# Attention output transposed by DMA from SBUF to SBUF, with the k and q loads placed behind it

## The chip, the cores and the metric

One core of a Trainium2 chip. The metric is the device time of one execution in microseconds (us). Engines: PE is TensorE, ACT ScalarE, DVE VectorE, POOL GpSimd, SP SyncE. Inputs and outputs lie in HBM, the tiles in SBUF, and matmuls write into PSUM. Spans are from one profiled execution of each kernel and lie up to 2 us below the device time of the same run. The granted clock is the share of its full clock that PE was given, 1.000 at most. "SPq" is SyncE as it issues DMAs. The chain is the work that ended last, followed back from the last instruction, at each step to what it had waited for.

## The reference, cut to what matters

```python
# 8 batches, 8 heads, 576 positions, head size 64; model 512, hidden 2048
scores = q @ k.T / 8 + bias[head, i - j]            # by distance; one value from |i - j| of about 128 on
attn   = softmax(scores)                            # 576 x 576 per head
x      = (attn @ v) as [batch * position, head * 64]     # 4608 x 512
h      = x @ w_in;  g = h + sin(alpha * h)**2 / alpha    # 4608 x 2048
out    = g @ w_out                                       # 4608 x 512
```

The kernel treats a batch as four pairs of heads, and the MoE part as nine blocks of 512 tokens. Batch t's attention and block t's MoE alternate.

## The kernel before

The first MoE product contracts over the model dimension, so x has to lie transposed, as `xT`, with the model dimension on partitions. The kernel makes it for each pair and each of two windows of positions (384 and 192): normalise on DVE (`xn`), transpose on PE into PSUM (`turn`), copy to `xT` on DVE or ACT (`put`).

```python
    XN = 1536                       # xT is a ring of 1536 token columns
    xT = sgl.tile([128, NP, XN], F16, name="xT")
    ...
        def turn(e):
            tr.v = new_av().bitcast(F16)
            for i, qc in enumerate(QC[w]):
                nc.tensor.transpose(out=tr.v[:, qc - q0 : qc - q0 + 128],
                                    in_=xn.v[:, i], identity=id_sb)
        ...
        def put(e):                 # PSUM -> xT, at (S * t + q0) % XN
            ...
```

k and q of the batches 2 to 7 are first cast by POOL's DMA into HBM ("staging"), then read back transposed by SyncE's DMA, a whole batch ahead of their use. k goes through `kraw` and from there, in four plain copies, to `kz` and `kt`.

```python
    def load_kqT(t):
        nc.sync.dma_start_transpose(out=kraw[:, :, :], in_=staged_k.ap()[t])
        kz = kzs[t % 2]
        nc.sync.dma_start(out=kz[0:64, :, 0:S], in_=kraw[0:64, :, :])
        nc.sync.dma_start(out=kz[64:128, :, S : 2 * S], in_=kraw[64:128, :, :])
        ...                         # two small copies to kts
        nc.sync.dma_start_transpose(out=qTs[t % 2][:, :, :], in_=staged_q.ap()[t])
    ...
        def first(t=t):             # with the first QK matmul of batch t
            if 1 <= t < T - 1:
                load_v16(t + 1)
                load_kqT(t + 1)
```

A scheduler in the program (`Plan`) fixes the order of every engine when the program is built, from its own table of durations. The second MoE product ("mo", 64 matmuls a block) is filler: the scheduler puts it where PE would wait, with a quota inside attention (`QUOTA = 48`, `OFFSET = 8`). On the chip every engine keeps the fixed order: PE's 3379 instructions in the experiments ring and ring_whole below, whose loads differ, come in the same order, one for one.

The softmax here doesn't subtract the row's maximum and nothing guards it: scores larger than these inputs give would overflow.

Of the kernel before, what the change touches and what calls it, by code (L numbers as in the profile page):

```python
# [24 lines left out]
def t_act(n):  # L25
    return n / 1200.0 + 0.052
# [4 lines left out]


D_TBL = 1.285
LAT = {"PE": 0.2, "ACT": 0.18, "DVE": 0.18, "POOL": 0.2, "DMA": 0.0}
NBUF = {"sc": 4, "av": 2, "mo": 2, "u": 2, "g": 2, "s16": 3, "sq": 3, "outs": 5, "xn": 3}


class Task:
    def __init__(self, engs, emit, deps, pri, nb=0.0):
        self.engs, self.emit, self.deps, self.pri, self.nb = engs, emit, list(deps), pri, nb  # L40
        self.allocs = []
        self.s_only = self.fill = False
        self.end = self.eng = None


class Buf:
# [8 lines left out]
class Plan:  # L55
# [18 lines left out]
    def ready(self, t):  # L74
        r = t.nb
        for d in t.after:
            if d.end is None:
                return None
        for d in t.deps:
            if d.end is None:  # L80
                return None
            r = max(r, d.end - (LAT["PE"] if d.eng == "PE" and "PE" in t.engs else 0.0))
        taken = {}
        for b in t.allocs:
            ring, n = self.rings[b.tag], NBUF[b.tag]
            k = taken[b.tag] = taken.get(b.tag, -1) + 1
            if len(ring) + k >= n:
                for x in ring[k - n].users:
                    if x.end is None:
                        return None  # L90
                    r = max(r, x.end)
        return r

    def run(self, t0):
        free = {e: t0 for e in ("PE", "ACT", "DVE", "POOL")}
        todo = list(self.tasks)
        while todo:
            best = None
            cands = {e: [] for e in free}
            look = 0  # L100
            for t in todo:
                look += 1
                if look > WINDOW:
                    break
                r = self.ready(t)
                if r is None:
                    continue
                for e in t.engs:
                    if e == "ACT" and t.s_only and not self.sin:
                        continue  # L110
                    st = max(free[e], r)
                    if t.fill:
                        if self.in_qk and self.used >= OFFSET + QUOTA * self.share:
                            continue
                        cands[e].append((st + FILL_GAP, t))
                    else:
                        cands[e].append((st, t))
            for e, c in cands.items():
                if not c:
                    continue  # L120
                s0 = min(x[0] for x in c)
                st, t = min(((x[0], x[1]) for x in c if x[0] <= s0 + SLACK[e]),
                            key=lambda x: (x[1].pri, x[0]))
                fin = st + t.engs[e]
                if best is None or (st, fin) < best[:2]:
                    best = (st, fin, e, t)
            st, fin, e, t = best
            if e == "PE" and self.warm is not None and free[e] < WARM_END:
                ring = self.rings["mo"][-2:]
                b = Buf("mo")  # L130
                x = Task({}, None, [], 0)
                b.users.append(x)
                if st > free[e] + 0.5 and len(ring) == 2 and all(
                    y.end is not None and y.end <= free[e] for y in ring[0].users
                ):
                    self.warm()
                    free[e] += 0.43
                    x.end, x.eng = free[e], e
                    self.rings["mo"].append(b)
                    continue  # L140
            if t.fill:
                self.used += 1
                st -= FILL_GAP
                fin -= FILL_GAP
            for b in t.allocs:
                self.rings[b.tag].append(b)
            t.emit(e)
            t.end, t.eng = fin + LAT[e], e
            free[e] = fin
            todo.remove(t)  # L150
        self.made = max(free.values())
# [12 lines left out]
T_TR1 = (38.5, 38.5)  # L164
T_W = 30.0
T_WO = 54.0
WARM0 = 6
WARM1 = 1
AV_PRI = 250
NORM_PRI = -300  # L170
CP_PRI = -1
SIN_SET = "trig_and_small"
SLACK = {"PE": 0.02, "ACT": 0.02, "DVE": 0.02, "POOL": 0.02}



# [11 lines left out]
def kernel(  # L188
# [11 lines left out]
    nc = tc.nc  # L200
    T, H, S, D = q.shape
# [11 lines left out]
    XN = 1536  # L213
# [8 lines left out]
    staged_k = nc.dram_tensor("staged_k", [T, S, H * D], F16, kind="Internal")  # L222
    staged_q = nc.dram_tensor("staged_q", [T, S, H * D], F16, kind="Internal")
# [112 lines left out]
                in_=src[t].rearrange("h s d -> s h d"),  # L336
            )

    def load_kqT(t):
        nc.sync.dma_start_transpose(out=kraw[:, :, :], in_=staged_k.ap()[t])  # L340
        kz = kzs[t % 2]
        nc.sync.dma_start(out=kz[0:64, :, 0:S], in_=kraw[0:64, :, :])
        nc.sync.dma_start(out=kz[64:128, :, S : 2 * S], in_=kraw[64:128, :, :])
        for z in range(2):
            r = slice(64 * z, 64 * z + 64)
            nc.sync.dma_start(out=kts[t % 2][r, :, r], in_=kraw[r, :, 512:S])
        nc.sync.dma_start_transpose(out=qTs[t % 2][:, :, :], in_=staged_q.ap()[t])

    def load_v16(t):
        vp = v[t].rearrange("h s d -> s h d")  # L350
# [76 lines left out]
    def load_mhr(eng):  # L427
# [12 lines left out]
        out=tabL,  # L440
# [107 lines left out]
    def plan_alpha():  # L548
# [13 lines left out]
        m = plan.add({"PE": 0.1}, mm, [], 5000, nb=20.0, new=[b])  # L562
        return plan.add({"DVE": 0.4}, cp, [m], 5000, use=[b])

    def plan_pair(t, p, kqt, tails, first, gate, ub):

        u = Cell()
# [3 lines left out]
        for i, (kind, c) in enumerate(units):  # L571
# [39 lines left out]
                         after=head, new=b + ([ub] if i == 0 else []))  # L611
            head = head or [m]
            x = plan.add({"ACT": t_act(n)}, ex, [m] + gate, base + 20, use=b + [ub])
            if kind == 1:

                def bh(e):
                    io = u.v[:, 8, 384:576]
                    nc.vector.tensor_tensor(out=io, in0=io, in1=mh[:, p, 0:192], op=ALU.mult)

                done[(0, 4)] = x  # L620
                done[(1, 4)] = plan.add({"DVE": 0.19}, bh, [x], base + 10,
                                         nb=0.0 if t else T_MH[p > 0], use=[ub])
                continue
# [22 lines left out]
    def plan_av(t, p, w, u, ub, done):  # L646
# [35 lines left out]

        x = plan.add({"DVE": 0.4 + n / 960.0}, norm, prev, base + NORM_PRI, new=[xb], use=[ab])

        def turn(e):
            tr.v = new_av().bitcast(F16)
            for i, qc in enumerate(QC[w]):
                nc.tensor.transpose(  # L688
                    out=tr.v[:, qc - q0 : qc - q0 + 128], in_=xn.v[:, i], identity=id_sb
                )  # L690
# [1 line left out]
        x = plan.add({"PE": 0.06 * nq}, turn, [x], base + NORM_PRI, new=[tb], use=[xb])  # L692

        def put(e):
            x0 = (S * t + q0) % XN
            for a, m in ((0, min(n, XN - x0)), (min(n, XN - x0), n)):
                if a < m:
                    copy_on(e, xT[:, p, (x0 + a) % XN : (x0 + a) % XN + m - a], tr.v[:, a:m])
# [97 lines left out]
    for t in range(T):  # L796
        PB = 1000000 * t

        def first(t=t):
            if 1 <= t < T - 1:  # L800
                load_v16(t + 1)
                load_kqT(t + 1)
            if t + 2 < T:
                stage_kq(t + 2)

        if t > 0:
            gate = [plan.add({"ACT": D_TBL}, lambda e: set_table(EXP_SET), sins, PB)]
        exps = []
        for p in range(NP):
            ub = Buf("u")  # L810
            if t == 0 and p + 1 < NP:
                for kq in range(2):
                    tr[(0, p + 1, kq)] = plan_tr(0, p + 1, kq, 100 * (16 * p + 8), T_PAIR[p][kq])
            kqt = tr[(t, p, 0)][0] + tr[(t, p, 1)][0] if t < 2 else []
            tails = tr[(t, p, 0)][1] if t < 2 else []
            u, done = plan_pair(t, p, kqt + pe_gate, tails, first, gate, ub)
            exps.extend(x for x in plan.tasks[-40:] if x.engs.keys() == {"ACT"})
            for w in range(2):
                xdone.setdefault((t, w), []).extend(plan_av(t, p, w, u, ub, done))
        if t == 0:  # L820
            for p in range(NP):
                for kq in range(2):
                    tr[(1, p, kq)] = plan_tr(1, p, kq, 20000 + 10 * p, T_TR1[kq])
        tbl = [plan.add({"ACT": D_TBL}, lambda e: set_table(SIN_SET), exps, PB)]
        sins = []
        for b in [t] if t < T - 1 else [t, t + 1]:
            m, s_ = plan_moe_in(b, tbl)
            sins += s_
        pe_gate = [m]
        for b in [t] if t < T - 1 else [t, t + 1]:  # L830
            for a in range(4):
                plan_mo(b, a)
# [33 lines left out]
```

## Time and profile before

| | before |
|---|---|
| device time, median of 2 | 416.26 us (414.1 to 418.43) |
| profiled span (of a further run, 412.09 us) | 410.3 us |
| PE, ACT, DVE busy | 96%, 82%, 71% |
| period of a batch (first MoE matmul to first MoE matmul, mean over batches 2 to 7) | 43.8 us |
| mean granted PE clock | 1.000 |

### The profile page before, as it was taken

The numbers are of one execution on the slowest core, as the hardware profiler recorded it, in microseconds if no ns is written. First come the engines' busy times: TensorE is split into PE (matmuls) and PEld (weight loads), VectorE is DVE, ScalarE is ACT, GpSimd is POOL, SyncE is SP. The second block draws the span as 40 slices with busy tenths as digits, with TensorE's granted clock in tenths as the row PEclk, the third lists the DMA queues.
The fourth block names the chain that finished last, engine by engine and source line by source line (L and its number), as shares of the span: only waits on it lengthen the run. The fifth ranks groups of instructions, "written<-read, shape, count | busy, mean of one in ns | idle before, by whom it ended". The sixth has DMA issues, their size and how long they took to land.

```text
span 410.3 us, 8747 instructions
## 1 busy us (share of the span) xinstructions
PE 395.4 (96%) x3519; PEld 227.5 (55%) x3519; DVE 289.7 (71%) x683; ACT 337.3 (82%) x502; POOL 85.6 (21%) x98
## 2 busy tenths in 40 slices
PE   4897999999999999999999999999999999999996
PEld 1474446754576447744665467645764477444442
DVE  5895996749666976688576956696768766799200
ACT  2877988879988998889888998799979988899311
POOL 7863952044000900071004400120000000000000
PEclk9999999999999999999999999999999999999999
DMA  9899999949900995099906990293000000000111
GB/s 170 189 206 219 205 162 158 216 89 164 185 28 29 155 182 94 27 135 165 131 28 104 161 142 27 69 169 79 27 28 27 26 27 27 28 1 0 53 77 77
DMA packets 135145, 41.90 MB, mean 102 GB/s; under 512 B 121209, under 2 KB 129489, under 8 KB 135105
## 3 DMA queue, kind: packets, MB, share of 16 engines
q0 software_dynamic: 89872, 19.04, 54.5%
q1 hardware_dynamic: 45008, 22.26, 24.2%
q8 instruction: 27, 0.44, 0.4%
q14 instruction: 14, 0.11, 0.1%
q10 hardware_dynamic: 224, 0.05, 0.1%
HBM read 37.76 MB, written 16.52 MB: 132 GB/s over the span
## 4 chain that ended last, share of the span: by engine, by line
PE 88%; DVE 8%; DMA 1%; ACT 1%; issue 1%; ACTq 0%; DVEq 0%
PE sc L408 44%; PE mo L408 30%; PE av L408 11%; PE av L688 2%; DVE kz L496 2%; DVE g L741 2%; DMA phi_sb<-phi_const 1%; DVE u L635 1%; DVE xn L678 1%; DVE qT L496 1%; ACT u L606 1%; DVE kt L542 1%; DVE sq L736 0%; PE mo L507 0%; PE mo L513 0%
## 5 line engine op out<-in xcount | busy, mean ns | idle before, releaser
L606 ACT ACTIVATE u<-sc 128x768 f16<-128x768 f32 (+1 forms) x224 | 165.9, 788 | 28.6 <-PE sc L408 23.5
L408 PE MATMUL mo<-w_out,g 128*128 128x512 f16 x576 | 156.5, 379 | 0.0
L408 PE MATMUL sc<-xT,w_in 128*128 128x512 f16 x576 | 131.2, 379 | 0.5 <-DVE g L741 0.5
L741 DVE SCALAR_TENSOR_TENSOR g<-sq,inv_a,sc 128x512 f16<-128x512 f16 x144 | 104.7, 747 | 7.8 <-ACT sq L734 4.9
L727 ACT ACTIVATE s<-sc,alphaT 128x512 f16<-128x512 f32 x144 | 92.4, 677 | 8.4 <-PE sc L408 7.3
L408 PE MATMUL sc<-qT,kz 128*128 128x192 f16 (+1 forms) x512 | 89.5, 288 | 2.0 <-ACT qT L494 0.7
L408 PEld LDWEIGHTS <-w_in 128*128 128x128 f16 x576 | 55.3, 98 | 64.7 <-issue 0.8
L635 DVE TENSOR_TENSOR u<-u,m2r 128x512 f16<-128x512 f16 (+1 forms) x192 | 70.5, 388 | 17.4 <-ACT u L606 14.9
L408 PEld LDWEIGHTS <-g 128*128 128x128 f16 x576 | 55.8, 98 | 45.2
L408 PEld LDWEIGHTS <-u 128*128 128x128 f16 x1440 | 55.2, 97 | 10.6 <-ACT u L606 2.5
L352 POOL DMA_DIRECT2D v<-in_v_dram x24 | 22.2, 1064 | 163.7 <-PE av L408 163.7
L408 PE MATMUL av<-v,u 128*128 128x65 f16 x1280 | 54.9, 193 | 0.5 <-DVE u L635 0.5
L408 PEld LDWEIGHTS <-kz 128*128 128x128 f16 x512 | 42.6, 98 | 22.0 <-issue 4.4
L734 ACT ACTIVATE sq<-s 128x512 f16<-128x512 f16 x79 | 49.4, 629 | 2.3
L677 DVE RECIPROCAL rd<-av 128x6 f32<-128x6 f32 x64 | 12.0, 188 | 38.1 <-PE av L408 38.1
L408 PE MATMUL av<-vh,u 128*128 128x130 f16 x160 | 35.2, 220 | 0.1
L678 DVE TENSOR_TENSOR xn<-av,rd 128x384 f16<-128x384 f32 x64 | 31.4, 491 | 2.2
L736 DVE TENSOR_TENSOR sq<-s 128x512 f16<-128x512 f16 x65 | 27.3, 421 | 2.9 <-ACT s L727 2.5
L496 DVE COPY outs<-mo 128x512 f32<-128x512 f32 x27 | 18.6, 690 | 10.9 <-PE mo L408 10.7
L688 PEld LDWEIGHTS <-xn 128*128 128x128 f16 x160 | 13.6, 98 | 18.0 <-DVE xn L678 6.4
L494 ACT ACTIVATE outs<-mo 128x512 f32<-128x512 f32 x9 | 5.4, 597 | 20.7 <-PE mo L408 20.7
L688 PE MATMUL av<-id_sb,xn 128*128 128x128 f16 x160 | 19.5, 220 | 2.9 <-DVE xn L678 2.8
(68 smaller groups left out, 185.6 us busy)
## 6 DMA issues: line engine op xcount, KB each, us to landing
out_dram<-outs SPq DMA_DIRECT2D x36, 256.0 KB, 2.0
staged_k<-in_k_dram POOLq DMA_DIRECT2D x6, 576.0 KB, 11.2
staged_q<-in_q_dram POOLq DMA_DIRECT2D x6, 576.0 KB, 17.5
kz<-kraw SPq DMA_DIRECT2D x12, 288.0 KB, 7.0
v<-in_v_dram POOLq DMA_DIRECT2D x24, 128.0 KB, 6.0
w_in<-in_moe_w_in_dram POOLq DMA_DIRECT2D x4, 512.0 KB, 8.5
w_out<-in_moe_w_out_dram POOLq DMA_DIRECT2D x4, 512.0 KB, 10.8
w_out<-in_v_dram SPq DMA_DIRECT2D x4, 256.0 KB, 9.1
```

Of the source, the lines that this page charges most:

```text
L352: nc.gpsimd.dma_start(out=vs[t % 2][:, c, :, 0:D], in_=vp[128 * c : 128 * c + 128],)
L408: nc.tensor.matmul(out=out, lhsT=lhsT, rhs=rhs, start=start, stop=stop)
L496: k_of(e).tensor_copy(out=o, in_=i)
L606: nc.scalar.activation(out=o, in_=x, func=AF.Exp, scale=0.125)
L635: nc.vector.tensor_tensor(out=io, in0=io, in1=m2[:, 2 * p : 2 * p + 2, x0 : x0 + hi - lo], op=ALU.mult,)
L677: nc.vector.reciprocal(out=r, in_=a[:, :, :, D])
L678: nc.vector.tensor_tensor(out=xn.v[:, 0:nq].rearrange("p c (z d) -> p c z d", z=2), in0=a[:, :, :, 0:D], in1=r.unsqueeze(3).to_broadcast([ ...
L688: nc.tensor.transpose(out=tr.v[:, qc - q0 : qc - q0 + 128], in_=xn.v[:, i], identity=id_sb)
L727: nc.scalar.activation(out=s16.v, in_=h.v, func=AF.Sin, scale=alphaT[:, f : f + 1])
L734: nc.scalar.activation(out=sq.v, in_=s16.v, func=AF.Square)
L736: k_of(e).tensor_tensor(out=sq.v, in0=s16.v, in1=s16.v, op=ALU.mult)
L741: nc.vector.scalar_tensor_tensor(out=gcell[b].v[:, f, :], in0=sq.v, scalar=inv_a[:, f : f + 1], in1=h.v, op0=ALU.mult, op1=ALU.add,)
```

## The change

The intent: 20 transposes a batch, and the copies behind them, leave PE, DVE and ACT and go to the DMA engines, which have little to do late in attention. All of them are put on SyncE's queue, where the k and q transposes are; and so that the k and q transposes (2.3 to 8.5 us of issue each in the trace before) do not stand in front of those of the running batch, the loads go behind them, in halves.

```diff
-LAT = {"PE": 0.2, "ACT": 0.18, "DVE": 0.18, "POOL": 0.2, "DMA": 0.0}
-NBUF = {... "xn": 3}
+LAT = {"PE": 0.2, "ACT": 0.18, "DVE": 0.18, "POOL": 0.2, "SP": 2.5}
+NBUF = {... "xn": 8}
 ...
+        if t > 0:
+            parts = []          # [block, first row, column of xT, rows, blocks]
+            ...                 # a part ends where the ring xT ends, and where windows overlap
+            def flip(e):
+                for i, row, c_, m, k_ in parts:
+                    ...
+                    nc.sync.dma_start_transpose(out=o, in_=src)
+            return [plan.add({"SP": 1.0 * len(parts)}, flip, [x], base + NORM_PRI, use=[xb])]
 ...
-                load_kqT(t + 1)
 ...
-            kqt = tr[(t, p, 0)][0] + tr[(t, p, 1)][0] if t < 2 else []
+            kqt = tr[(t, p, 0)][0] + tr[(t, p, 1)][0] if t < 2 else loads
 ...
+        if 1 <= t < T - 1:
+            for y in range(2):  # halves of k; behind the last transpose of batch t
+                x = plan.add({"SP": 3.0}, ...load_T(kraw, staged_k.ap()[u_], y)...,
+                             xdone[(t, 0)] + xdone[(t, 1)], ...)
+                x.lag = 4.0
+            ...                 # the four copies to kz and kt, then two halves of q
```

More of the change, by code (lines that the diff above doesn't have):

```diff
@@ L33 @@
 D_TBL = 1.285
-LAT = {"PE": 0.2, "ACT": 0.18, "DVE": 0.18, "POOL": 0.2, "DMA": 0.0}
-NBUF = {"sc": 4, "av": 2, "mo": 2, "u": 2, "g": 2, "s16": 3, "sq": 3, "outs": 5, "xn": 3}
+LAT = {"PE": 0.2, "ACT": 0.18, "DVE": 0.18, "POOL": 0.2, "SP": 2.5}
+NBUF = {"sc": 4, "av": 2, "mo": 2, "u": 2, "g": 2, "s16": 3, "sq": 3, "outs": 5, "xn": 8}
 class Task:
@@ L43, in __init__ @@
         self.end = self.eng = None
+        self.lag = 0.0
 class Buf:
@@ L81, in ready @@
                 return None
-            r = max(r, d.end - (LAT["PE"] if d.eng == "PE" and "PE" in t.engs else 0.0))
+            r = max(r, d.end + d.lag - (LAT["PE"] if d.eng == "PE" and "PE" in t.engs else 0.0))
         taken = {}
@@ L94, in run @@
     def run(self, t0):
-        free = {e: t0 for e in ("PE", "ACT", "DVE", "POOL")}
+        free = {e: t0 for e in ("PE", "ACT", "DVE", "POOL", "SP")}
         todo = list(self.tasks)
@@ L166 @@
 T_WO = 54.0
+T_L1 = 68.0
 WARM0 = 6
@@ L172 @@
 SIN_SET = "trig_and_small"
-SLACK = {"PE": 0.02, "ACT": 0.02, "DVE": 0.02, "POOL": 0.02}
+SLACK = {"PE": 0.02, "ACT": 0.02, "DVE": 0.02, "POOL": 0.02, "SP": 0.02}
 def _bucket_table(max_abs: int) -> np.ndarray:
@@ L337, in stage_kq, with load_T, load_kz @@
             )
-    def load_kqT(t):
-        nc.sync.dma_start_transpose(out=kraw[:, :, :], in_=staged_k.ap()[t])
+    def load_T(dst, src, y):
+        nc.sync.dma_start_transpose(out=dst[:, 2 * y : 2 * y + 2, :],
+                                    in_=src[:, 256 * y : 256 * y + 256])
+    def load_kz(t):
         kz = kzs[t % 2]
@@ L346, in load_kqT @@
             nc.sync.dma_start(out=kts[t % 2][r, :, r], in_=kraw[r, :, 512:S])
-        nc.sync.dma_start_transpose(out=qTs[t % 2][:, :, :], in_=staged_q.ap()[t])
     def load_v16(t):
@@ L563, in plan_alpha @@
         return plan.add({"DVE": 0.4}, cp, [m], 5000, use=[b])
+    exs = {}
     def plan_pair(t, p, kqt, tails, first, gate, ub):
@@ L613, in plan_pair @@
             x = plan.add({"ACT": t_act(n)}, ex, [m] + gate, base + 20, use=b + [ub])
+            exs.setdefault((t, p), x)
             if kind == 1:
@@ L683, in plan_av @@
         x = plan.add({"DVE": 0.4 + n / 960.0}, norm, prev, base + NORM_PRI, new=[xb], use=[ab])
+        x0 = (S * t + q0) % XN
+        if t > 0:
+            parts = []
+            for i, qc in enumerate(QC[w]):
+                lo = 0 if i == 0 else QC[w][i - 1] + 128 - qc
+                a = (x0 + qc - q0 + lo) % XN
+                k_ = min(128 - lo, XN - a)
+                for row, c_, m in ((lo, a, k_), (lo + k_, 0, 128 - lo - k_)):
+                    if m == 128 and parts and parts[-1][3] == 128 and parts[-1][2] + 128 * parts[-1][4] == c_:
+                        parts[-1][4] += 1
+                    elif m:
+                        parts.append([i, row, c_, m, 1])
+            def flip(e):
+                for i, row, c_, m, k_ in parts:
+                    o = xT[:, p, c_ : c_ + m * k_]
+                    if k_ > 1:
+                        o = o.rearrange("d (b q) -> d b q", b=k_)
+                        src = xn.v[row : row + m, i : i + k_].rearrange("q b d -> q (b d)")
+                    else:
+                        src = xn.v[row : row + m, i]
+                    nc.sync.dma_start_transpose(out=o, in_=src)
+            return [plan.add({"SP": 1.0 * len(parts)}, flip, [x], base + NORM_PRI, use=[xb])]
         def turn(e):
@@ L694, in put @@
         def put(e):
-            x0 = (S * t + q0) % XN
             for a, m in ((0, min(n, XN - x0)), (min(n, XN - x0), n)):
@@ L819 @@
                 xdone.setdefault((t, w), []).extend(plan_av(t, p, w, u, ub, done))
+        if 1 <= t < T - 1:
+            u_ = t + 1
+            loads = []
+            for y in range(2):
+                x = plan.add({"SP": 3.0}, lambda e, u_=u_, y=y: load_T(kraw, staged_k.ap()[u_], y),
+                             xdone[(t, 0)] + xdone[(t, 1)], PB + 100 + y, nb=T_L1 if t == 1 else 0.0)
+                x.lag = 4.0
+                loads.append(x)
+            kz_ = plan.add({"SP": 2.6}, lambda e, u_=u_: load_kz(u_), loads[:], PB + 200)
+            kz_.lag = 2.0
+            loads = [kz_]
+            for y in range(2):
+                x = plan.add({"SP": 3.0},
+                             lambda e, u_=u_, y=y: load_T(qTs[u_ % 2], staged_q.ap()[u_], y),
+                             xdone[(t, 0)] + xdone[(t, 1)], PB + 150 + y, nb=T_L1 if t == 1 else 0.0)
+                x.lag = 4.0
+                loads.append(x)
         if t == 0:
```

## The prediction

> **What bounds the kernel now.** I read the table of busy time first, then the slices, then the chain of waits, then one steady batch in the timeline of PE (TensorE) and of ACT (ScalarE). Page of the kernel before, busy time and the PE row of the slices:
>
> ```profile
> PE 395.4 (96%) x3519; PEld 227.5 (55%) x3519; DVE 289.7 (71%) x683; ACT 337.3 (82%) x502; POOL 85.6 (21%) x98
> PE   4897999999999999999999999999999999999996
> ACT  2877988879988998889888998799979988899311
> ```
>
> PE never rests between the third slice and the last. The chain agrees, and puts a figure on the transposes (L688):
>
> ```profile
> PE 88%; DVE 8%; DMA 1%; ACT 1%; issue 1%; ACTq 0%; DVEq 0%
> PE sc L408 44%; PE mo L408 30%; PE av L408 11%; PE av L688 2%; DVE kz L496 2%; DVE g L741 2%; DMA phi_sb<-phi_const 1%; DVE u L635 1%; DVE xn L678 1%; DVE qT L496 1%; ACT u L606 1%; DVE kt L542 1%; DVE sq L736 0%; PE mo L507 0%; PE mo L513 0%
> ```
>
> "sc" is both the QK products and the first MoE product, "mo" the second MoE product, "av" the product with v. The windowed chain of one batch shows the real cost per matmul (start, us, what):
>
> ```profile
> 88.69 5.18 PE sc L408 x24
> ...
> 106.18 1.08 PE mo L408 x5
> ...
> 112.11 0.17 PE av L688 x3
> ...
> 114.73 0.11 PE av L688 x2
> ```
>
> So a 512-column matmul costs 0.216 us (5.18/24, 1.08/5), and the five transposes of a pair 0.28 us, not 5 x 0.22: the 220 ns of their row overlap. The first MoE matmul comes at 88.69 us in batch 1 and at 219.07 in batch 4; the batches in between are alike, with a period of 43.77 us.
>
> The second thing to see is why PE is never idle although ACT is needed for every score. ACT's timeline in batch 4's attention:
>
> ```profile
> 193.51 4.55 ACT L606 ACTIVATE u<-sc 128x768 f16<-128x768 f32 x6
> 198.71 1.51 ACT L606 ACTIVATE u<-sc 128x768 f16<-128x768 f32 x2 [0.65 <-PE sc L408]
> ...
> 217.16 0.81 ACT L606 ACTIVATE u<-sc 128x768 f16<-128x768 f32 x1 [0.64 <-PE sc L408]
> 217.99 1.28 ACT L789 ACT_TABLE_LOAD   x1
> ```
>
> A batch has 28 exponentials. Starts inside an unbroken run lie 0.745 us apart for 768 columns and about 0.61 for 576, so a pair's seven need 6 x 0.745 + 0.61 = 5.08 us and a batch 20.3 us, at least. QK and AV of a batch are only 8.64 us (20736 columns a batch at 0.216 us per 512) and 6.0 us (0.90 + 0.60 per pair) of PE. PE is full in that stage because 56 of the batch's 64 mo matmuls (12 us) are interleaved there, seen in the instruction order of PE. That interleaving is the thing to watch.
>
> **What the Trainium skill says.** "VectorE: DVE Perf Modes", section "The three transpose paths", gives a 128x128 bf16 transpose 390 ns on TensorE and 1309 ns by DMA. The trace's TensorE figure is lower: 219 ns of latency and 54 ns of PE when back to back. "DMA: Bandwidth & Descriptors", section "Latency and other measured facts", speaks of about 2 us of fixed cost of a DMA; the trace agrees, the 256 KB output stores land after 2.0 us. The same page's "Rules for kernel authors" says that a DMA which reads what an earlier DMA wrote must wait for its completion; the k path (transpose to kraw, then copies to kz) does so and pays two landings. The page "Advanced Engine Details and Errata", "X-Bar Transpose (TRN2)", says such DMAs are as fast as regular ones; this trace has only transposes from HBM:
>
> ```profile
> out_dram<-outs SPq DMA_DIRECT2D x36, 256.0 KB, 2.0
> kz<-kraw SPq DMA_DIRECT2D x12, 288.0 KB, 7.0
> kraw<-staged_k SPq DMA_TRANSPOSE x6, 7.6
> qT<-staged_q SPq DMA_TRANSPOSE x6, 11.3
> 231.66 8.54 SPq L347 DMA_TRANSPOSE qT<-staged_q  x1
> 275.26 2.85 SPq L347 DMA_TRANSPOSE qT<-staged_q  x1
> ```
>
> The last two lines are the issue of the same transfer with the DMA engines full of the staging of k and q (8.54 us) and without it (2.85 us; the fastest q landed after 4.9 us). A 128x384 piece of xn is a sixth of it. My estimate, from these: 0.5 to 1 us of issue, landing 2.5 to 3 us after xn is ready.
>
> **Part by part, per batch from 1 to 7.**
>
> (a) Removed: 20 transposes, 4 x 0.28 = 1.1 us of PE, in all 7.8 us (1.9%), which is nearly all on the path; also the PSUM copies to xT on DVE and ACT (47 and 21 of them, 0.25 to 0.5 us), off the path. If nothing else happened: 402 us of span.
>
> (b) Added before the first MoE matmul: it needs window 0 of the last pair (window 1 too in batch 1). Before, the step from xn to xT was a transpose and a copy with PE filled by mo matmuls. Now it is a DMA, and in the new PE order no mo matmul is left there: "AV 27, QK 4, AV 18, MoE-in 24".
>
> (c) Moved: k and q loads. Before, they are issued a whole batch ahead (kraw at 176.72 us for a batch that starts at about 235). Now they stand behind all transposes of batch t and are for batch t+1. The scheduler thinks that they land late, so it gives PE everything it has while it waits. In the order the run of mo matmuls between MoE-in and the first QK of the next batch becomes 24, 41, 41, 41, 33, 41 (for the batches 1 to 6); before it was 4 or 5. The batch's remaining 20 or so mo matmuls come in the first two pairs, and the last two pairs have none. Engines execute in order, so this holds on the chip whether the loads land early or not.
>
> So two stages that overlapped become serial: a MoE stage bound by PE with ACT idle for its last third, and an attention stage bound by ACT with PE idle.
>
> MoE stage, from its first matmul to the first QK: 64 + 3 + 41 = 108 matmuls x 0.2165 = 23.4 us (91 after batch 1: 19.7; 100 after batch 5: 21.65).
>
> Attention stage, from first QK to first MoE-in matmul:
> - 0.55 us from QK to the first exponential (0.33 us of matmul, 0.2 of hand-over; the function table was loaded during the mo run).
> - 20.3 us of exponentials, plus gaps. The gap of 0.65 us before the seventh exponential comes where 27 AV matmuls stand ahead of its QK; the new order keeps this in three pairs of four: 1.95, and some 0.5 of smaller ones. 22.8 us.
> - From the last exponential to MoE-in. In the trace the AV run of window 0 ends 0.95 us after the fifth exponential's end, xn is written 1 us later, and the last exponential ends 2.25 us after the fifth. With 2.5 to 3 us for the DMA, MoE-in starts 2.4 us after the last exponential.
>
> Sum 25.75 us. Period 23.4 + 25.75 = 49.15 us in place of 43.77: 5.4 us longer, the 1.1 us saved being already in it.
>
> The whole, as starts of MoE-in: batch 1 at 91.3 (88.69, less about 0.6 for its transposes, plus 3.2 for two more DMA pieces and their landing); batch 2 after 19.7 + 26.5 (40 mo matmuls still in it, so nearer to PE's bound) at 137.5; batches 3, 4, 5 at 186.6, 235.8, 284.9; batch 6 after 21.65 + 25.75 at 332.3; batch 7 at 381.5. From there to the end before: 410.3 - 350.4 = 59.9, now 59.6. Span 441, that is 31 us more. On the median of 416.3 this gives 447; the profiled run of before lay lower (412.1), so I say 446.
>
> **Rivals.**
> 1. The gain stays: PE remains full, 402 us of span, some 408 by the clock. For it: transposes lie on PE's chain, and PE is 96% busy. Against it: the order just read. Even with no gap between exponentials, 2 us at the end, and 0.5 at the start, a period is 23.4 + 22.8 = 46.2, still 2.4 longer; six such stages leave the span near 421, 2.6% up. That is my floor.
> 2. The loads set the pace: kraw takes 7.6 us, the q halves up to 8.5 of issue under staging, the kz copies 7 more. Behind the last transpose (about 2.5 us after the end of AV) that is 21 us after the end of AV; PE asks for them 1 + 23.4 us after it. I think they are in time by 3 us, but in batches 1 to 4 staging runs in the same stretch (DMA share above 1 in those windows, below 0.1 in the later attention), and batch 1 has only 24 mo matmuls to cover it. If they are 4 us late, add 4 to each of four batches: about 460.
> 3. The transposes block SyncE's queue: about two or three for each pair, with output stores between them that wait for DVE. If each piece takes 4 us or more to land, only the last one of the batch is waited for, so 1.5 us more per batch, 10 in all: 456. Against it: by the end of attention the staging is over.
>
> **Range and chances.** The floor of 421 of span is 427 by the clock, and takes every gap away; late loads give 460. Between them 432 to 460 should hold 8 in 10. Faster by 2% needs PE full throughout, which the order excludes: 0.02. Within 2% needs periods under 45.3, below my floor: 0.04. Slower: 0.94.
>
> **What would show it.** In the changed profile: PE's share falls to about 88%, with idle time put down to ACT (exponentials) in the last two pairs of each batch and to the xT transpose before MoE-in; a mo run of about 9 us before each QK from batch 3 on; ACT's exponentials nearly unbroken over about 23 us; a period of 49 us; the idle time after that mo run small. I am wrong if the first QK waits for kz or qT by more than 1 us (rival 2), if MoE-in waits over 2 us for xT (rival 3), or if PE shows no idle time in attention (rival 1).

## The result, and the profile after

| | before | changed |
|---|---|---|
| device time, median | 416.26 us | 462.53 us (460.74 and 464.32) |
| profiled span | 410.3 us | 462.5 us |
| PE, ACT, DVE busy | 96%, 82%, 71% | 89%, 71%, 63% |
| mean granted PE clock | 1.000 | 0.978 |

The ratio is 1.111 (95% interval 1.080 to 1.142). Ratios are the mean time of one kernel's fast runs over that of the other's fast runs of the same rounds, so not quite the ratio of the medians. A second set of six runs gave 460.54 us and 1.112 (1.106 to 1.118), so it is 11% slower: the direction of the forecast, and 16.5 us beyond the time that it gave.

The page of the changed kernel: busy time, the PE slices, the granted clock in tenths, the shares of the chain that ended last by engine, and the row of the new transposes (count, median us from issue to landing):

```profile
PE 410.4 (89%) x3379; PEld 224.3 (48%) x3379; DVE 291.8 (63%) x647; ACT 328.3 (71%) x478; POOL 85.5 (18%) x98
...
PE   5998979969998999799978998369988998799996
...
PEclk9998989989999999999999999969999999999999
...
PE 70%; ACT 10%; DMA 8%; DVE 7%; issue 3%; SPq 2%; ACTq 0%
...
xT<-xn SPq DMA_TRANSPOSE x96, 2.3
```

PE was 88% of the chain and is now 70%; ACT, DMA and SyncE's queue have 20% together (2% before). PE's busy time is *higher* although it has 140 transposes fewer; busy does not mean useful here, and some of it is matmuls that take longer, as the chain shows below. And the dents in the PE row are not alike: one slice, the 26th, falls to 3 tenths, and the next has the lowest clock, 6 tenths. Something happens once.

The chain in order of time (start, us, what; x21 are the 21 matmuls of the first MoE product that wait for the last `xT`):

```profile
147.53 4.69 PE sc L412 x21
...
161.50 8.85 PE mo L412 x41
...
194.15 2.35 DMA xT<-xn
...
196.55 4.69 PE sc L412 x21
...
300.37 4.45 DMA xT<-xn
...
304.87 6.87 PE sc L412 x21
```

The second line is the run of 41 mo matmuls of the forecast, 8.85 us of filler in one piece. 196.55 less 147.53 is a period of 49.02 us. Here are all starts of that group against the forecast. (The forecast's starts are those of the first MoE matmul. On the chip three matmuls, 0.65 us, run before this group, as they need only the first three pairs; so some 0.65 us of each difference is in the definition.)

| batch | forecast start | measured start | forecast period | measured period |
|---|---|---|---|---|
| 1 | 91.3 | 100.28 | | |
| 2 | 137.5 | 147.53 | 46.2 | 47.25 |
| 3 | 186.6 | 196.55 | 49.1 | 49.02 |
| 4 | 235.8 | 245.96 | 49.2 | 49.41 |
| 5 | 284.9 | 304.87 | 49.1 | **58.91** |
| 6 | 332.3 | 354.87 | 47.4 | 50.00 |
| 7 | 381.5 | 403.84 | 49.2 | 48.97 |
| end | 441 | 462.5 | 59.5 | 58.7 |

Of the 21.5 us missed, 9.0 come before batch 1's MoE and 9.8 in batch 5. What batch 5 does is in PE's timeline (in brackets: idle time just before, and what ended it) and in SyncE's:

```profile
304.87 6.87 PE L412 MATMUL sc<-xT,w_in 128*128 128x512 f16 x21 [9.36 <-DMA xT<-xn]
```

```profile
280.85 26.08 SPq L713 DMA_TRANSPOSE xT<-xn  x20
...
342.93 14.22 SPq L713 DMA_TRANSPOSE xT<-xn  x8
```

PE stands still for 9.36 us. SyncE issues 20 transposes in a row for 26.08 us, 1.30 us for each, with at most 0.11 us between them until the last `xT` of this MoE: it is behind, and issue is what it is behind with. (The row of 8 in batch 6 takes 1.78 us for each and has pauses of up to 1.7 us in it.) The last `xn` that this MoE needs was written at 292.95, its last transpose was issued at 300.37, 7.4 us later, and landed after 4.45 us in place of 2.4: about 7.3 us of the wait are the backlog and 2.1 a slow landing. Batch 5 has 24 transposes and the other batches 12, since its window 0 begins at token 2880, column 1344 of a ring of 1536; the ring ends 192 columns later, in the middle of a block of 128, and each pair's transposes are cut there into four pieces instead of one.

The repeat has the same batch 5 (period 58.8; the other five average 49.2). In it, batch 4's exponentials on ACT begin and end as follows:

```profile
217.43 4.52 ACT L612 ACTIVATE u<-sc 128x768 f16<-128x768 f32 x6 [7.13 <-PE sc L412]
...
240.35 0.81 ACT L612 ACTIVATE u<-sc 128x768 f16<-128x768 f32 x1 [0.65 <-PE sc L412]
```

From 217.43 to 241.16 are 23.73 us for 28 exponentials; the forecast was 22.8. ACT sat idle for 7.13 us before them, in the mo run. The 21 matmuls then began at 243.27, 2.1 us after the last exponential; the forecast was 2.4.

### The profile page after: what moved, and what is told of

The parts are those of the page before. It is cut to its first block, busy times and chain, and to the rows that moved or that the text cites. A ratio compares the mean times of both kernels' runs of the same rounds, so it can differ in the third digit from the quotient of the medians.

```text
span 462.5 us, 8624 instructions
## 1 busy us (share of the span) xinstructions
PE 410.4 (89%) x3379; PEld 224.3 (48%) x3379; DVE 291.8 (63%) x647; ACT 328.3 (71%) x478; POOL 85.5 (18%) x98
## 3 DMA queue, kind: packets, MB, share of 16 engines
q0 software_dynamic: 89872, 19.04, 49.3%
## 4 chain that ended last, share of the span: by engine, by line
PE 70%; ACT 10%; DMA 8%; DVE 7%; issue 3%; SPq 2%; ACTq 0%
PE sc L412 37%; PE mo L412 22%; PE av L412 10%; ACT u L612 9%; DMA xT<-xn 4%; DMA kz<-kraw 3%; DVE g L772 2%; DVE kz L500 2%; SPq L713 1%; DVE kt L546 1%; DVE xn L685 1%; DVE natx L420 1%; PE mo L517 1%; SPq L347 0%; PE mo L511 0%
## 5 line engine op out<-in xcount | busy, mean ns | idle before, releaser
L412 PE MATMUL sc<-xT,w_in 128*128 128x512 f16 x576 | 137.4, 391 | 15.3 <-DMA xT<-xn 14.4
L412 PE MATMUL mo<-w_out,g 128*128 128x512 f16 x576 | 144.3, 382 | 0.0
L412 PE MATMUL sc<-qT,kz 128*128 128x192 f16 (+1 forms) x512 | 92.1, 296 | 17.1 <-ACT u L612 13.2
L412 PEld LDWEIGHTS <-w_in 128*128 128x128 f16 x576 | 56.8, 100 | 86.5 <-DMA xT<-xn 15.1
L412 PEld LDWEIGHTS <-g 128*128 128x128 f16 x576 | 56.5, 98 | 58.8 <-issue 1.0
L412 PEld LDWEIGHTS <-kz 128*128 128x128 f16 x512 | 44.5, 100 | 44.3 <-issue 25.8
L412 PE MATMUL av<-v,u 128*128 128x65 f16 x1280 | 57.4, 194 | 7.6 <-DVE u L642 7.2
L356 POOL DMA_DIRECT2D v<-in_v_dram x24 | 22.2, 1065 | 194.4 <-PE sc L412 194.4
L765 ACT ACTIVATE sq<-s 128x512 f16<-128x512 f16 x73 | 45.6, 629 | 2.1
L767 DVE TENSOR_TENSOR sq<-s 128x512 f16<-128x512 f16 x71 | 29.7, 419 | 25.6 <-ACT s L758 25.6
L336 POOL DMA_DIRECT2D staged_q<-in_q_dram x6 | 16.1, 2685 | 1.5 <-DMA staged_q<-in_q_dram 1.5
```

Source lines behind the costliest of these rows:

```text
L336: nc.gpsimd.dma_start(out=dst.ap()[t].rearrange("s (h d) -> s h d", h=H), in_=src[t].rearrange("h s d -> s h d"),)
L356: nc.gpsimd.dma_start(out=vs[t % 2][:, c, :, 0:D], in_=vp[128 * c : 128 * c + 128],)
L412: nc.tensor.matmul(out=out, lhsT=lhsT, rhs=rhs, start=start, stop=stop)
L765: nc.scalar.activation(out=sq.v, in_=s16.v, func=AF.Square)
L767: k_of(e).tensor_tensor(out=sq.v, in0=s16.v, in1=s16.v, op=ALU.mult)
```

## The experiments

Two theories of the 21 us missed were tested first. The **cut theory**: the ring's end cuts batch 5's transposes into 24, at 1.21 us of issue each on SyncE (the median of the repeat; the shortest took 1.09) that is 29 us for some 24 us of exponentials. The **load theory** (the forecast's second rival): the k and q loads are late, or wait behind the transposes. Later experiments took apart the 31 us that had been forecast. Medians are of the device times of all runs; "clock" is the mean granted PE clock of the profiled run; the period is the mean over batches 2 to 7. All ratios are against the kernel before in the same rounds, where its median was 414.8 to 415.2 us.

| kernel | median us | ratio (95%) | period | clock |
|---|---|---|---|---|
| changed, again | 460.54 | 1.112 (1.106 to 1.118) | 51.4 | 0.977 |
| ring | 446.54 | 1.076 (1.069 to 1.082) | 49.3 | 0.984 (1.00 from 105 us on) |
| ring_whole | 447.50 | 1.078 (1.075 to 1.081) | 49.1 | 0.988 |
| early | 438.67 | 1.057 (1.052 to 1.063) | 46.0 | 0.969 |
| late_pe | 437.19 | 1.054 (1.048 to 1.059) | 47.8 | 1.000 |
| double | 536.59 | 1.296 (1.285 to 1.308) | 62.0 | 0.903 |
| blind | 473.79 | 1.133 (1.123 to 1.142) | 53.0 | 0.967 |
| early_warm | 433.52 | 1.045 (1.041 to 1.048) | 45.4 | 0.990 |
| early_t2 | 442.20 | 1.066 (1.062 to 1.071) | 49.2 | 0.973 |
| early_q32 | 423.51 | 1.024 (1.018 to 1.030) | 45.2 | 0.994 |
| early3b | 414.10 | 0.999 (0.994 to 1.005) | 43.8 | 0.994 |
| early3b_q46 | 409.60 | 0.985 (0.981 to 0.990) | 42.9 | 0.998 |

All gave the reference's result.

### again and ring: the changed kernel repeated, and without the cut

```diff
-    XN = 1536
+    XN = 3584           # ring only
```

With 3584 columns the ring ends inside no pair of blocks of batch 5. Batch 5 then has 12 transposes; a cut falls in batch 6, which has 16.

> The changed kernel again, unaltered. Theory A (stages made serial: about 5 us in each of the periods 2 to 7, plus 10 us in batch 5 for 24 transposes in SyncE's queue, plus a few us of waits in batch 1): ratio 1.10, and the first MoE matmul of batch 1 near 92 us if the 8 us lost in batch 0 of the first profile were chance (a slower PE clock at the start). If those 8 us belong to the change, it comes near 100 us again and the ratio is 1.11 or more.

> The ring xT 3584 columns long instead of 1536, so that batch 5 is not cut by its end: 12 transposes there and not 24 (batch 6 gets 16). Theory A: the wait of 9.4 us before the MoE matmuls of batch 5 falls to about 1 us, and the time is 8 to 10 us below the run 'again'. Rival (that wait comes from the load of the DMA engines, not from the number of transposes in the queue): less than 2 us.

The issue of the transposes in the repeat (min/median/max in ns), and the chain of the repeat and then of ring, at batch 5:

```profile
L713 SPq DMA_TRANSPOSE xT<-xn x96: 1093/1208/2040, 71.0 to 401.6; - x96
```

```profile
297.53 4.48 DMA xT<-xn
...
302.05 6.34 PE sc L412 x21
```

```profile
289.82 2.35 DMA xT<-xn
...
292.21 4.69 PE sc L412 x21
```

Ring comes 9.84 us sooner to this point, 9.2 us of it in batch 5, and the 21 matmuls take 4.69 us, not 6.34: after the long wait they had run at a clock of 0.50. That makes 10.9 us, as much as the two profiled spans differ; the medians differ by 14.0 us. So the cut is worth 11 to 14 us (the last 3 are in no trace), and the loads, which ring leaves as they are, are not the cause of that part. The repeat started batch 1 at 95.80 us, between the two cases of its expectation. Ring's profiled run counted as slow, just over 1.5% above the fastest of its six; the records show a lower clock in its first 105 us only and full clock in the batches quoted here. But batch 1 began at 96.20 us, as late as in the repeat.

### double: 24 transposes in every batch

```diff
-                k_ = min(128 - lo, XN - a)
+                k_ = 64 if w == 0 and i == 0 else min(128 - lo, XN - a)
```

On ring, with blocks no longer merged, so that window 0 of every pair is cut into four.

> As ring, but window 0 of each pair cut into four transposes, so that every batch from 1 to 7 has 24 of them, as batch 5 had. If SyncE's queue at about 1.2 us a transpose is what cost batch 5 its 9 us, each of the periods becomes 57 to 60 us and the time 500 to 510 us. Rival (batch 5 is slow for another reason, its place in the ring or its output stores): within 10 us of ring.

The list of waits (us in total, times, longest):

```profile
PE sc L412 <- DMA xT<-xn: 77.3, 12, 9.1
```

536.59 us, beyond what was expected (two runs only, so no verdict by the 2% rule, but far outside any spread seen). The sign holds: every batch waits now, as batch 5 alone did, 7.1 to 16.1 us. The size does not: the period grew by 12.7 us, where batch 5 had lost 9.8. QK waited for no load (the list of waits has none). In the batches 1 to 4 the transpose that ended the wait landed after 5.9 to 6.7 us; from batch 5 on it took 2.3 to 3.0, and there the periods are 57.2 and 56.7 us, about as expected. The clock fell to 0.903; the run doesn't separate what that adds.

### early and late_pe: one part of the change each

Early is ring with the k and q loads as they were before, whole and a batch ahead. Late_pe is the changed kernel with the loads late, but the transposes on PE (and 3 `xn` buffers, as before).

```diff
# early
-        if 1 <= t < T - 1:
-            for y in range(2):  ...      # the block of late loads
+                load_kqT(t + 1)          # back in first()
-            kqt = ... if t < 2 else loads
+            kqt = ... if t < 2 else []
# late_pe
-        if t > 0:
+        if False:                        # no flip: PE transposes
```

> As ring, but k and q loaded whole and a batch ahead, as before the change; the transposes stay on DMA. Theory A: the mo matmuls are back among the exponentials, a period is 43 to 44.5 us, and the ratio to before is 0.995 to 1.02. Rival B (the transposes by DMA themselves are the cost, by latency and by the queue): periods of 47 us or more, ratio above 1.06.

> Transposes back on PE, k and q loads still in halves and behind the attention. Theory A: the run of 40 mo matmuls before QK stays, and periods are 47 to 49 us, ratio 1.06 to 1.08. Rival B: about 1.00 to 1.02.

Either part alone costs 22 to 24 us, and both together (ring) 32: the costs do not add up. In the traces early's period is 2.2 us over before, but ring's only 1.5 over late_pe's, and the wait in batch 1 is 9.9 us in early and 4.6 in ring; why the two parts share so much is not shown. Early missed both cases of its expectation (period 46.0, ratio 1.057), if nearer to the rival. Late_pe runs at full clock, and its chain has:

```profile
232.36 5.18 PE sc L412 x24
...
244.02 8.63 PE mo L412 x40
```

The 40 mo matmuls in one piece are there without any DMA transpose. They come from the late loads: the scheduler thinks that k and q land late and pours its filler in while it waits. It is the mechanism of the forecast, and its period of 47.8 us is 4.0 above before; five of these and 2.3 us in the period before them make 22, as in the medians (22.2).

Early has no such run, and its transposes all the same cost 23.7 us: five periods of 2.23 us more are 11.2, and batch 1 waited 9.9 us for `xT`, with a slow group after it (6.84 us). SyncE's timeline and the chain of early show where:

```profile
71.42 6.47 SPq L361 DMA_TRANSPOSE qT<-staged_q  x1
...
78.62 3.75 SPq L723 DMA_TRANSPOSE xT<-xn  x3
```

```profile
95.01 8.14 DMA xT<-xn
...
196.11 6.39 PE sc L422 x21
...
243.21 4.69 PE sc L422 x21
```

In batch 1 a q transpose holds SyncE for 6.47 us ahead of the first transpose of `xn`; it is what the change put the loads behind the transposes for. But by the last one, issued at 95.01, SyncE is only 1.8 us behind (its `xn` was written at 93.24), and most of the wait is the landing, 8.14 us in place of 2.3. POOL's loads of v had begun 2.2 us before that issue. In ring and the changed kernel they began 0.5 us before it, and the last transpose of batch 1 landed after 4.4 to 4.5 us; whether they are the cause is not shown. The other thing is the last two lines: 6.39 us and 4.69 us for the same 21 matmuls, in turn from batch to batch. Two windows of 1 us at the first of them (PE, PEld, DVE, ACT and POOL busy, PE clock, DMA share, GB/s) give the clock:

```profile
196.00:197.00 1.00, 0.89 (x3) 0.42 (x4) 0.00 (x0) 0.41 (x1) 1.00 (x2) 0.65 0.63 42
197.00:198.00 1.00, 1.00 (x3) 0.30 (x2) 0.65 (x2) 0.28 (x1) 1.00 (x2) 0.50 1.97 153
```

PE is busy and runs at half its clock. Before it lay two gaps of 0.86 us (waiting for the last `u` of DVE) and 1.02 us (for `xT`):

```profile
193.54 0.60 PE L422 MATMUL av<-v,u 128*128 128x65 f16 x6 [0.86 <-DVE u L652]
...
196.11 6.39 PE L422 MATMUL sc<-xT,w_in 128*128 128x512 f16 x21 [1.02 <-DMA xT<-xn]
```

The batches 2, 4 and 6 had the same gaps within 0.1 us, and their groups kept the full clock (4.69 us); why every second one falls is open. What this costs was to be measured by itself.

### early_warm: early, with work for PE in the gap

```diff
+                for _ in range({1: 40}.get(b, 5) if f == 0 and 0 < b < T else 0):
+                    full(h.v, zz[:, 0:128], zz, True, True)   # zeros, result unused
```

> As early, with idle time of PE before the MoE stage filled by matmuls on zeros whose result is overwritten (40 in batch 1, 5 in each later one; the first three MoE matmuls run before the wait). They add no waiting if they fit in the idle time. If the granted clock falls because PE was idle, the first 21 MoE matmuls take 4.7 us in every batch (6.2 to 6.8 in every second batch of early), the clock over the span is 0.98 or more, and the time is 5 to 9 us below early. If the dips have another cause, it is equal to early or up to 3 us above.

433.52 us: 5.2 less than early, though PE does more. The period is the same in every batch, 45.4, and the long groups of 21 are gone from the steady batches. The first 21 MoE matmuls of the batch shown for early are now:

```profile
193.52 4.82 PE L422 MATMUL sc<-xT,w_in 128*128 128x512 f16 x21
```

The gap of 0.87 us is still there, and the one before the group is filled. In batch 1, where PE still waited 6.06 us, the group took 6.25 us. So an idle gap does lower the clock, and filling it pays. "TensorE: Matmul & The Clock Gate", section "Part 1: The HAM clock gate (the "warmup" mystery)", in the Trainium skill, says that the clock halves after an idle window of about 3.4 us and comes back after as long a busy one. The half clock agrees, 0.50 in the window above. In early no idle time of 3.4 us was needed: the two of about 1 us, with PE busy between them, came before each lowered group of the steady batches.

### ring_whole and blind: do the halves, or the scheduler, matter?

Ring_whole loads k and q in one piece each, not two, in the same PE order as ring. Blind leaves SyncE as in ring, but tells the scheduler that the loads have landed, so that PE's order is that of early.

```diff
# blind
-            kqt = ... if t < 2 else loads
+            kqt = ... if t < 2 else []
```

> As ring, with k and q each loaded by one transpose and not in halves; PE's order is the same, instruction for instruction. If the halves matter, QK waits for the loads by some us in the batches 2 to 5 and the time is 5 us or more above ring; if not, within 3 us of ring.

> As ring in what SyncE is told to do, but the scheduler takes the loads for landed, so PE's order is, instruction for instruction, that of early, with 4 mo matmuls between the MoE-in stage and QK in place of 41. It differs from early only in when the loads are issued. Loads landed about 24 us after the end of AV in again; here PE asks for them some 18 us after it: waits of 5 to 7 us for kz and qT in the batches 2 to 5 and 0 to 2 us later, time 20 us above early in these and less in batch 1, so 442 to 455 us in all. If the loads were not what mattered but only the order, it is equal to early within 1%.

The halves do not matter: 1.078 and 1.076, with overlapping intervals. Blind was to part the late loads from the order of PE. It was slower than its expectation (442 to 455 us) and than ring, 1.133 against 1.076 (three of its six runs slow; the ratio uses the other three). PE's timeline in blind:

```profile
219.00 0.50 PE L412 MATMUL sc<-qT,kz 128*128 128x384 f16 x2 [1.60 <-DMA qT<-staged_q]
...
225.94 0.50 PE L412 MATMUL sc<-qT,kz 128*128 128x384 f16 x1 [4.93 <-DMA kz<-kraw]
```

QK now really waits for the loads, 1.60 and 4.93 us. So the scheduler was right: loads behind the last transpose do land late, and a run of filler is the better answer to it. With PE's order the same, one instruction for one, blind's period is 53.0 us and early's 46.0: what costs is the place of the loads on SyncE.

### early3b, early_t2 and early_q32: which transposes cost?

All have the loads early and batch 1 on PE. Early_t2 transposes all pairs of the batches 2 to 7 by DMA; early3b only the pairs 0 to 2, the last pair by PE; early_q32 is early_t2 with a smaller quota of mo matmuls inside attention, so that 18 are left between the last product with v and MoE.

```diff
-        if t > 0:                       # early
+        if t > 1:                       # early_t2, early_q32
+        if t > 1 and p < NP - 1:        # early3b
-    QUOTA = 48
+    QUOTA = 32                          # early_q32 only
```

> As early, but batch 1 keeps its transposes on PE; batches 2 to 7 have all of theirs on DMA. In early, the transposes of batch 1 stood behind the loads of batch 2 in SyncE's queue and PE waited 9.9 us for them. If that was the queue's order, this is 10 to 13 us below early (426 to 430 us), and what it still lies above early3b (10 to 15 us) is the price of the last pair's transposes, 2 us or so in each of six periods. If the wait in batch 1 only moves to batch 2, it is within 4 us of early.

> Loads a batch ahead, transposes by DMA only for pairs 0 to 2 of batches 2 to 7; the last pair, which the MoE stage waits for, on PE. Theory: what is left of the cost in early is the latency behind the last pair (about 2 us a period, and a slower PE clock after it) and batch 1, where loads stand ahead of the transposes in the queue. Then a period is 42.9 to 43.2 us and the ratio 0.98 to 1.00. Rival (any DMA transpose beside attention costs, by DMA or SBUF contention): ratio above 1.02.

> Loads a batch ahead, all transposes of batches 2 to 7 by DMA, and 18 mo matmuls kept for the time between the last AV of window 0 and the MoE stage (3 in early). They last 3.9 us, about as long as xn to xT by DMA. Theory: the wait and the slow clock after it go, a period is 42.7 to 43.2 us, ratio 0.98 to 1.00. Rival (the mo matmuls are missed among the exponentials, where they had filled PE): 44.5 us or more a period, ratio above 1.02.

Early3b is as fast as before, 0.999. Taking the one last pair back to PE turns 1.066 into 0.999, so with early loads, the cost of the transposes is in the pair that MoE waits for, together with the clock and the order of PE that come with it. But where is the gain? The period stayed at 43.8 us (42.9 to 43.2 expected). From the first QK to the first MoE matmul it took 0.43 us less than before (27.30 and 27.73; the transposes of three pairs take 0.84), and from there to the next QK 0.42 more. (The expectation of early3b_q46 has 0.65 and 0.4, which would not leave the period unchanged.) Early3b's chain there:

```profile
222.77 0.69 DVE outs L510
223.46 0.28 DVE xT L510
```

The PSUM copy to `xT` of the last pair now stands behind an output copy on DVE.

Early_t2 missed its expectation: the wait in batch 1 went, as it should, yet it was no faster than early. In five of six batches PE waited 2.5 to 3.1 us for the last transpose (early: 1.0), which landed after 3.9 to 4.4 us where the trace has the landing (early: 2.4), and in those five the 21 matmuls took 6.0 to 7.6 us. From its chain:

```profile
228.00 4.36 DMA xT<-xn
```

The order on every engine is that of early from batch 2 on. In both, POOL's loads of v start about 1 us after the transpose, and one of the late ones, in batch 6, has no such load near it. Why it lands later is open.

Early_q32 tested whether filler in front of MoE hides the landing. It does, nearly: MoE waited 0.70 us at most, the 21 matmuls took 4.7 us in every batch, and the ratio is 1.024. But its period of 45.2 us is that of the rival in the expectation. ACT in early_q32, first and last exponential:

```profile
199.13 4.45 ACT L622 ACTIVATE u<-sc 128x768 f16<-128x768 f32 x6
...
221.99 0.81 ACT L622 ACTIVATE u<-sc 128x768 f16<-128x768 f32 x1 [0.65 <-PE sc L422]
```

That is 23.67 us with 37 mo matmuls among the exponentials. It was 24.46 before (193.51 to 217.97) with 44, 25.36 in early with 50, and the changed kernel takes 23.73 with only 20. So much filler does lengthen the stage, but from 37 down to 20 nothing is won: there ACT's exponentials, with some 3.2 us of gaps between them, set its length, and filler that leaves it comes on top behind it.

### early3b_q46: a version that beats both

Early3b with a quota of 46, which the scheduler turns into seven mo matmuls ahead of MoE, and puts the copy to `xT` on DVE in front of the output copy.

```diff
-    QUOTA = 48
+    QUOTA = 46
```

> As early3b, with 2 mo matmuls fewer allowed among the exponentials, which puts the output copy of the last mo group on DVE behind the xT copy of the last pair and leaves 7 mo matmuls, not 3, before the MoE stage. In early3b 0.65 us of the 0.84 us of transposes per batch was won in attention and 0.4 lost again at the start of the MoE stage, where the xT copy stood behind an output copy on DVE. If that copy is what ate it, the period falls from 43.77 to 43.0 to 43.4 us and the ratio is 0.985 to 0.995. If PE's freed time is simply lost to the pace of the exponentials, the period stays at 43.7 us or more and the ratio at 1.00.

```profile
PE 390.0 (97%) x3429; PEld 222.2 (55%) x3429; DVE 286.4 (71%) x658; ACT 333.9 (83%) x488; POOL 85.6 (21%) x98
```

409.60 us, ratio 0.985 (0.981 to 0.990), as expected: less than 2%, but clear of 1. The period is 42.9 us. PE is 97% busy with 5.4 us less to do. Ninety fewer instructions on PE (3429 in place of 3519) are the 15 transposes of each of six batches; at 0.28 us per five they are worth 5.0 us, and the kernel won 5.6. The kernel before was not run with a quota of 46, so a part of the gain could be the quota's. It does act by itself: from early3b to early3b_q46 ACT's idle time among the exponentials of a batch falls from 4.4 to 3.25 us. That is where it stood before, too (3.2).

## Why the prediction was right or wrong

**Direction: right, and by its own mechanism.** PE's share is 89% (88 said). The order of PE was read correctly, and late_pe shows the 40 mo matmuls in one piece as the result of the late loads alone. The two serial stages have the predicted lengths: exponentials 23.7 us (22.8 said), last exponential to MoE 2.1 (2.4), the period in batches 3, 4 and 7 49.0 to 49.4 (49.1 to 49.2). The first rival (gain kept) fell, as foreseen; the second fell too, in the kernel as changed: QK waited 0.74 us for `kz` at most in the repeat. Blind shows how close it was: it is the long mo run that hides the loads. The third is the one whose sign came, MoE waiting over 2 us for `xT` (9.36 us in batch 5, 4.49 in batch 1), though it was to come by slow landings.

**Size: wrong by 16.5 us, and the step that failed is the wait for the transposes: their count and their price on SyncE's queue.** The forecast's sum charges each batch one landing ("With 2.5 to 3 us for the DMA, MoE-in starts 2.4 us after the last exponential"). Behind it stand "0.5 to 1 us of issue" in its estimate of a piece and "about two or three for each pair" in its third rival, where at worst "only the last one of the batch is waited for". Measured were 1.21 us (median; 1.09 at the least), and in batch 5 six for each pair. Twenty-four times 1.21 are 29 us of SyncE, more than the 23.7 us of exponentials; then not the last one alone is waited for but the whole backlog, 9.36 us of standing PE. The estimate took a sixth of the issue of a large transposing load; the issue does not shrink with the size that way: a piece of 128x384 took 1.20 us and one of 64x128 1.22. The cut could have been read in the diff and counted in the order of SyncE: 2880 modulo 1536 is 1344, and 1536 less 1344 is not a multiple of 128. This term is shown by ring, 11 us in the traces and 14.0 in the medians.

**A missing term: the clock.** The forecast priced every matmul at 0.216 us, and it made PE idle. The group of 21 took 6.3 to 7.1 us where PE had stood, not 4.69: 1.6 to 2.4 us in each of the batches 1 and 5. For batch 5 it lies inside ring's difference (6.87 in place of 4.69 is also most of what made batch 6's period 50.0 instead of 47.4). Early_warm shows by itself that the term exists, 5.2 us there.

**Batch 1: started 9.0 us late** in the profiled run and 4.5 in the repeat (95.80). The forecast had 3.2 us for two more pieces and their landing; in the profiled run the last one landed after 4.38 us and PE waited 4.49. The rest is partly chance of the start: in both runs one copy of k, 64x64 on DVE, took 1.85 us in place of 0.18, ahead of batch 1's first QK, and the clock was low there. Such a copy, of 1.7 to 1.9 us, is in seven of the fourteen profiled runs, with early3b among them, and in the others the longest took 0.6 to 1.4 us; and early_t2, which has early3b's order on PE up to 129 us, is one of them. What decides it stays open.

**Without the cut the forecast's 446 is met** (446.54, ratio 1.076 against 446/416.26 = 1.071). That is the mechanism, with some luck: batch 1 is late by 4.9 us in ring too (96.20), and the base was 1 us lower in those rounds.

**The other part of the forecast's sum,** the saving of 1.1 us a batch, is borne out where nothing waits for the DMA: early3b_q46 won 5.6 us with three quarters of it, if the quota's own part is small.

**Small slips of the forecast,** on which nothing rests: 20736 columns at 0.216 us per 512 are 8.75 us, not 8.64; of the 47 and 21 copies to `xT`, 43 and 17 go, as batch 0 keeps its own; a transpose behind another takes 56 ns of PE, not 54; and it is the fourth MoE matmul that needs the last pair, not the first.

## What to carry to other kernels

Work taken from a busy engine was won here only where nothing waits for its replacement: three of four pairs could go to DMA, and the last one, which the next stage waits for, could not. Count DMA instructions, not bytes, on the queue that issues them: here a piece of 64x128 cost as much issue as one of 128x384, and the place where a ring buffer wraps decides how many there are. When a scheduler fills gaps by its own durations, read the new order of every engine first; and an engine that is made to wait briefly may also run slower afterwards.

## What the Trainium skill lacked or had wrong

- "VectorE: DVE Perf Modes", "The three transpose paths", has one time for each way (390 ns on TensorE, 1309 ns by DMA). Neither decides: on PE a transpose costs 56 ns back to back, and by DMA each instruction from SBUF to SBUF costs a median of 1.21 us of SyncE's issue, landing after a median of 2.3 us. I found no page with the issue time of one such DMA; the one table in cycles, in "DMA: Bandwidth & Descriptors", sets a later chip against "previous generations" without naming them. It bound batch 5.
- "Advanced Engine Details and Errata", "X-Bar Transpose (TRN2)", calls such DMAs as fast as regular ones. From issue to landing that agrees (2.3 us against 2.1 for the output stores, which are larger), but the issue of a store took a median of 0.34 us and that of a transpose 1.21.
- "TensorE: Matmul & The Clock Gate", the section named above, puts the halved clock down to an idle window of about 3.4 us. Here gaps of 0.86 and 1.02 us, with PE busy between, came before it in every second batch; the 21 matmuls took 6.39 in place of 4.69 us, and filling the second gap won 5.2 of 438.7 us, 1.2%. The page's "A second HAM failure mode: psum-queue depth-cycling" does know of short idles that make the clock swing, but gives no length for them.
- I found no page that tells of a 64x64 copy on DVE taking 1.7 to 1.9 us in place of 0.18, as it did in seven of fourteen profiled runs; it is not explained.
